# Attention with a top-32 mask and a maxout layer on one core: the first batch's values loaded later, their zero blocks written once, and new estimates in the planner

## The chip, the cores and the metric

The kernel runs on one core of one Trainium2 chip. A core has five engines that work side by side, each through its own list of instructions in the order in which they were written down: TensorE (PE, matrix products), VectorE (DVE), ScalarE (ACT), GpSimd (POOL) and SyncE (SP, which here only issues transfers, DMAs, between HBM and the on-chip memory). An instruction that waits for another engine holds up everything behind it on its own engine. The metric is the device time of one execution in microseconds (us).

## The reference

```
scores = q @ k^T / 8                       # 8 batches x 8 heads, 576 queries, 576 keys, 64 wide
kth    = 32nd largest score of each row
attn   = softmax(scores where scores >= kth, else -1e9)
x      = attn @ v                          # heads side by side: 4608 tokens x 512
h      = max(x @ w1, x @ w2, x @ w3)       # 512 -> 768
out    = h @ w_out                         # 768 -> 512
```

All inputs and the output are float32. The kernel splits float32 numbers into a high and a low half of 16 bits (or a rounded and a remaining part), and makes three products of halves where one float32 product is asked for.

## The kernel before, in words

**Attention.** A batch has four pairs of heads. For a pair, `load_qk` loads queries and keys by six DMAs; `prep` turns them on PE (lines 451 and 460), ACT brings them back (454, 464, 465) and POOL takes the remaining part (469). The 576 queries of a pair are five units: four of 128 queries for both heads and one of 64. A unit goes through some twenty steps: scores on PE (L508), copies by ACT (L519), the eight largest of each group of 72 scores on DVE (L536), a guess at the 32nd largest (L542 to L567), a sign pass on ACT (L574), a product on POOL (L579), a maximum pass on DVE (L583), the mask on DVE (L626), the exponential on ACT (L635), turned weights on PE (L693) and copies by ACT (L708). Every two units, PE multiplies the weights with the values (`values`, L738) and DVE scales the result (`scaled_x`, L748).

**Values.** `load_v` fills a tile `vt` of 128 x 10 x 64 numbers for a pair of heads by six DMAs from HBM (lines 400 to 405). Two half blocks of the tile must be zero, and two further DMAs (406, 407) copy them there from a tile `zeros`, at every load. `square_v` (ACT, L414) sums the squares of the values of each pair; when all four pairs of a batch are summed, `scale_v` makes the scale that L748 needs: a sum on DVE (L180), a product on PE (L184), a copy by ACT (L188) and three small steps on DVE (`powers`, 165 to 169).

**Weights.** 18 blocks of `w1`, `w2`, `w3` and `w_out` are loaded (L227), decoded by DVE in 30 pieces of three instructions (L240 to L242), squared by ACT (L252), summed by PE (L261), and cut into 16-bit halves in 48 pieces (POOL L298, ACT L301, POOL L304). From the second group of blocks on, a load needs the decoding of the block four places earlier.

**Expert layer.** For each batch, PE multiplies x with the three inner weights (L794) and h with the outer ones (L854). These products need all the weight cuts of their block and x of all four pairs. Their instructions stand in a second list, `fill`, from which the planner takes when PE has nothing better.

**The planner.** Every step is a `Piece` with an engine, an estimated duration, the pieces that it needs, and a rank. `in_order` simulates the five engines with these estimates and writes the pieces down one by one. For each engine it looks at pieces by rank (the window reaches `LEAD` = 8 ranks above the lowest that is left), and takes among those the first in rank whose estimated start is within `PATIENCE` of the earliest (0 for SP and ACT). A result is taken to be seen by another engine after the piece's duration plus `LATE` of the piece's engine plus 100 ns. So estimates, ranks and `LATE` set the order of each engine's list, and nothing else: on the chip the engines wait for each other by semaphores.

Unit n has rank n plus the offset of the step in `OFFSETS`; the loads of queries and keys have the rank of their first unit minus 3.5 (-3.5, -1.5, 0.5, 2.5 for the four pairs of the first batch, whose first units are 0, 2, 4, 6). Weight group i has rank `RANK_W[i]`, its loads at most `RANK_W[2]`. Loads of values have the rank of their pair's first unit plus `RANK_V` = -12.

Of the kernel before, what the change touches and what calls it, by code (L numbers as in the profile page):

```python
# [8 lines left out]
F32 = mybir.dt.float32  # L9
# [23 lines left out]
LEAD = 8.0  # L33
LOCK_A = -150.0
LOCK_B = -100.0
OFFSETS = {'x1': 0.96, 'j': 0.85, 'i': 0.48, 'N': 0.29, 'w1': -0.04, 'e1': -1.15, 'y': 0.91, 's1': 0.01, 'v': -0.12, 'u': -0.09, 'p1': -0.14, 'g0': 0.06}
RANK_P = -3.5
RANK_R = 4.0
AHEAD = 4
RANK_W = (-2.0, 1.0, 3.0, 5.0)  # L40
RANK_V = -12.0
RANK_M = -20.0
LATE = {'PE': 160.0, 'DVE': 85.0, 'ACT': 100.0, 'POOL': 40.0, 'SP': 2000.0}


class Piece:
# [86 lines left out]
def kernel(ctx, tc, q, k, v, moe_w1, moe_w2, moe_w3, moe_w_out, out):  # L133
    nc = tc.nc
    B, H, S, D = q.shape
    P = 128
# [11 lines left out]
    const = ctx.enter_context(tc.tile_pool(name="const", bufs=1))  # L148
    io = ctx.enter_context(tc.tile_pool(name="io", bufs=2))
# [63 lines left out]
    def load_weight(j):  # L213
        src, c, n, at0 = parts[j]
        if c % 2 == 0:
            raw = [wall.bitcast(I32)[:, 2 * CUT + at0:2 * CUT + at0 + 2 * n]]
        elif j < 3 * KC:
            raw = [wk.tile([P, n], I32, name=nm) for nm in ("xh", "xl")]
        elif j == len(parts) - 1:
            raw = [wk.tile([P, 2 * n], I32, name="ssb", bufs=NSSB)]  # L220
        elif j in raw_of:
            raw = raw_of[j]
        else:
            raw, raw_of[j + 2] = ([wk.tile([P, 2 * n], I32, name=nm)] for nm in ("xh", "xl"))
        m = 2 * n // len(raw)
        for k, t in enumerate(raw):
            nc.sync.dma_start(t, src[c * P:(c + 1) * P, :].bitcast(I32)[:, k * m:(k + 1) * m])  # L227
        raw_of[j] = raw
# [84 lines left out]
    def piece(engine, cost, run, needs=(), rank=0.0, takes=(), mode=None, alone=False):  # L313
        x = Piece(engine, cost, run, needs, rank, [(rings[r], rel) for r, rel in takes], mode, alone)
        pieces.append(x)
        return x

    def scale_pieces(parts_, needs, rank):
        a = piece("DVE", 55, parts_[0], needs, rank)
        rel = []  # L320
        b = piece("PE", 64, parts_[1], [a], rank, [("tr", rel)])
        c = piece("ACT", 40, parts_[2], [b], rank)
        rel.append(c)
        return piece("DVE", 200, parts_[3], [c], rank)
# [3 lines left out]
    def weights():  # L328

        decoded, loads, last_cut, staged_odd = {}, {}, [], []  # L330
        for i in range(4):
            mine = range(i * KC, (i + 1) * KC) if i < 3 else range(3 * KC, len(parts))
            rank = RANK_W[i]
            done = []
            release = []
            for j in mine:
                n = parts[j][2]

                free, c = [], parts[j][1]
                takes = [] if c % 2 == 0 else [("ssb", free)] if j == len(parts) - 1 else [("x", free)]  # L340
                needs = [decoded[j - AHEAD]] if j >= AHEAD else []
                if c % 2 and 3 * KC + 1 < j < len(parts) - 1:
                    takes, free = [], staged_odd[-1]
                    needs.append(loads[j - 2])
                loads[j] = piece("SP", 4100 if i < 3 else 2700, lambda j=j: load_weight(j), needs, min(rank, RANK_W[2]), takes)
                if c % 2:
                    staged_odd.append(free)
                    if j < len(parts) - 1:
                        before_x.append(loads[j])
                for j0 in range(0, n, PIECE[n]):  # L350
                    rel = []
                    x = piece("DVE", 1300 if i < 3 else 1800, lambda j=j, j0=j0: decode(j, j0),
                              [loads[j], *([decoded[j - 1]] if j else []), *([x] if j0 else [])], rank, [("ob", rel), ("ob", rel)])
                    rel.append(x)
                decoded[j] = x
                free.append(x)
                rel = []
                y = piece("ACT", 740, lambda j=j: square_w(j), [x], rank, [("junk", rel)])
                if i < 3:
                    z = piece("PE", 330, lambda j=j: sum_w(j), [y, *done[-1:]], rank, [("m", release)] * 2 if j % KC == 0 else [])  # L360
                    rel.append(z)
                    done.append(z)
                else:
                    rel.append(y)
                    done.append(y)
            if i < 3:
                scaled = piece("DVE", 1500, lambda i=i: column_scale(i), done, rank)
                release.append(scaled)
            else:
                scaled = scale_pieces(norm_scale("wo", lambda: wosq, const), done, rank)  # L370
                wo_scaled.append(scaled)
            for j in mine:
                for j0 in range(0, parts[j][2], CUT):
                    f = cut(j, j0)
                    rel = []
                    a = piece("POOL", 450, f[0], [scaled], rank, [("ws", rel)])
                    h = piece("ACT", 410, f[1], [a, *last_cut], rank)
                    lo = piece("POOL", 630, f[2], [h], rank)
                    rel.append(lo)
                    last_cut = [a, h]  # L380
                    lows[j, j0] = lo
# [2 lines left out]

    v_of, vs_of, sq_of, qk_of, T_of, at = {}, {}, {}, {}, {}, {}

    zeros = const.tile([P, D], F32, name="zeros")
    nc.gpsimd.memset(zeros, 0.0)


    def main_rows(t, b, h):
# [2 lines left out]
    def load_v(b, hp):  # L394


        vt = io.tile([P, 10, D], F32, name="vt", bufs=6)
        v0, v1 = (main_rows(v, b, 2 * hp + h) for h in range(2))
        last = v[at.get(b, b), 2 * hp:2 * hp + 2, MAIN:S]
        nc.sync.dma_start(vt[:, 0:NU, :], v0)  # L400
        nc.sync.dma_start(vt[0:64, 8, :], last[0])
        nc.sync.dma_start(vt[0:64, NU:2 * NU, :], v1[64:P])
        nc.sync.dma_start(vt[64:P, NU:2 * NU - 1, :], v1[0:64, 1:NU])
        nc.sync.dma_start(vt[64:P, 2 * NU - 1, :], last[1])
        nc.sync.dma_start(vt[64:P, 9, :], v1[0:64, 0])
        nc.sync.dma_start(vt[64:P, 8, :], zeros[64:P])
        nc.sync.dma_start(vt[0:64, 9, :], zeros[0:64])
        v_of[b, hp] = vt

    def square_v(b, hp):  # L410
# [5 lines left out]
    def scale_v(b):  # L416
        return norm_scale("v", lambda: sq_of.pop(b), sm, lambda: vs_of.update({b: scale_of["v"]}))
# [586 lines left out]
    scaled_v, loaded_v = {}, {}  # L1004
# [4 lines left out]
    def values_of(b):  # L1009

        done = []
        first = min(k for k, x in enumerate(units) if x[0] == b)
        for hp in early if b == 0 else range(NP):
            at_ = units.index((b, hp, 0))
            v_done[b, hp] = []
            x = loaded_v[b, hp] = piece("SP", 1600, lambda hp=hp: load_v(b, hp), rank=at_ + RANK_V, takes=[("vt", v_done[b, hp])])
            rel = []
            y = piece("ACT", 910, lambda hp=hp: square_v(b, hp), [x], first - 1.0, [("junk", rel)])
            rel.append(y)
            v_done[b, hp].append(y)  # L1020
            done.append(y)
        scaled_v[b] = scale_pieces(scale_v(b), done, first + 0.5)

    load_last, users = [], [[] for _ in preps]

    def prepare(pi):
        b, hp = preps[pi]
        rank = starts[pi] + RANK_P
        load = piece("SP", 3200, lambda: load_qk(b, hp), list(load_last), rank)
        box = {}  # L1030
        load_last.clear()
        done, last = [], list(load_bits)
        load_bits.clear()
        for k in range(3):
            def products(k=k):
                if k == 0:
                    box["turns"] = prep(b, hp)
                box["turns"][k][0]()
            rel = []
            x = piece("PE", 109 if k == 0 else 436, products, [load, *done[-1:]], rank, [("tr", rel)])  # L1040
            y = piece("ACT", 157 if k == 0 else 1100, lambda k=k: box["turns"][k][1](), [x, *last, *done[-1:]], rank)
            rel.append(y)
            load_last.append(x)
            if pi >= 2:
                users[pi - 2].append(x)
            done.append(y)
            if k:
                z = piece("POOL", 1364, lambda k=k: box["turns"][k][2](), [y], rank)
                done.append(z)
                load_bits.append(z)  # L1050
        prepared[pi] = done
# [60 lines left out]
    with tc.If(redo != 0):  # L1112
        with tc.For_i(0, B, 1) as b:
# [6 lines left out]
            for hp in range(NP):  # L1120
# [5 lines left out]
                for u in range(NU + 1):  # L1126
                    i = len(units)
# [52 lines left out]
```

## Time and profile before

| | |
|---|---|
| median of 3 runs | 1386.01 us (1384.56 to 1386.39) |
| profiled execution, device time | 1387.35 us |
| profiled execution, span from first to last instruction | 1385.6 us |
| PE busy | 1225.9 us (88%) |
| DVE busy | 1202.1 us (87%) |
| ACT busy | 1118.7 us (81%) |
| POOL busy | 992.7 us (72%) |
| mean granted TensorE clock | 0.965 |

The busy times are over the whole span, whose parts differ: the first 200 us hold the decoding of the weights beside the attention of the first units, then follows a long steady part, and the last 70 us hold the expert layer's end. A granted clock of 1.00 stands for TensorE's upper level (2.4 GHz), 0.50 for its lower one (1.2 GHz).

### The profile page before, as it was taken

How to read it: one execution, taken by the hardware profiler on the slowest of the kernel's cores; microseconds unless marked ns; L12 is line 12 of the kernel's file. 1: busy time of each engine (PE TensorE's matmuls, PEld its weight loads, DVE VectorE, ACT ScalarE, POOL GpSimd, SP SyncE). 2: the span in 40 equal slices, each digit the busy share in tenths (PEclk: the TensorE clock that was granted, in tenths of full speed). 3: DMA queues.
4: the chain of work that ended last, by engine and by line, in shares of the span. 5: the costliest groups of instructions: out<-in, count | busy, mean ns of one | idle time of the engine just before them, and what ended most of it. 6: DMA issues, size and time to landing. Idle time of an engine off the chain costs nothing.

```text
span 1385.6 us, 32482 instructions
## 1 busy us (share of the span) xinstructions
PE 1225.9 (88%) x9981; PEld 867.2 (63%) x9981; DVE 1202.1 (87%) x5928; ACT 1118.7 (81%) x2732; POOL 992.7 (72%) x1658
## 2 busy tenths in 40 slices
PE   0434489899889999999999999999999999999997
PEld 0222257577557676776667675777677766767775
DVE  1899689989989999999999899999999999999621
ACT  2556689988998889988997899899988998898622
POOL 1589877778776778777877787788777887777511
PEclk9997589989879999999999999999999999999999
DMA  4541001110110010101010201111111101000000
GB/s 145 172 139 52 1 18 36 49 41 19 52 28 18 26 45 19 43 19 53 19 53 1 68 21 33 29 46 26 36 37 34 45 23 37 19 17 1 17 17 26
DMA packets 113014, 54.75 MB, mean 40 GB/s; under 512 B 96960, under 2 KB 105152, under 8 KB 112832
## 3 DMA queue, kind: packets, MB, share of 16 engines
q1 hardware_dynamic: 112832, 52.59, 14.1%
q8 instruction: 81, 1.33, 0.4%
q14 instruction: 101, 0.83, 0.2%
HBM read 42.07 MB, written 9.44 MB: 37 GB/s over the span
## 4 chain that ended last, share of the span: by engine, by line
PE 58%; DVE 19%; ACT 13%; issue 3%; SPq 3%; POOL 3%; DMA 1%; ACTq 0%; DVEq 0%; POOLq 0%
PE m L794 24%; PE tr L738 9%; PE s L508 9%; PE tr L693 7%; PE m L854 6%; DVE L L536 5%; DVE ssb L626 3%; ACT pm L635 3%; DVE Q L583 2%; ACT pT L708 2%; ACT ssb L519 2%; ACT w L574 2%; DVE ob L241 2%; PE tr L460 1%; DVE wall L242 1%
## 5 line engine op out<-in xcount | busy, mean ns | idle before, releaser
L794 PE MATMUL m<-xh,wall 128*128 128x256 f16 (+2 forms) x2448 | 441.2, 280 | 1.2 <-DVE h L803 0.6
L579 POOL TENSOR_TENSOR w<-ssb,w 128x576 f32<-128x576 f32 x288 | 413.4, 1440 | 29.2 <-ACT w L574 25.2
L794 PEld LDWEIGHTS <-wall 128*128 128x128 f16 x3672 | 340.0, 98 | 85.7 <-issue 15.9
L794 PE MATMUL m<-xl,wall 128*128 128x256 f16 (+2 forms) x1224 | 336.0, 279 | 0.0
L536 DVE MAX8 L<-s 128x8 f32<-128x72 f32 x2048 | 306.3, 220 | 20.2 <-PE s L508 10.3
L626 DVE SCALAR_TENSOR_TENSOR ssb<-ssb,kth 128x576 f32<-128x576 f32 x288 | 262.0, 925 | 1.1
L635 ACT ACTIVATE pm<-ssb,nb 128x576 f32<-128x576 f32 x288 | 224.2, 779 | 44.2 <-DVE ssb L626 40.6
L508 PE MATMUL s<-kT,qT 64*128 64x288 f32 x1920 | 216.5, 338 | 30.5 <-ACT ssb L519 8.7
L574 ACT ACTIVATE w<-ssb,Q 128x576 f32<-128x576 f32 x288 | 222.9, 778 | 13.9 <-DVE Q L567 10.8
L693 PE MATMUL tr<-ident,pm 128*128 128x128 f32 x1152 | 186.6, 290 | 52.8 <-ACT pm L635 47.8
L583 DVE MAX8 Q<-w 128x8 f32<-128x576 f32 x288 | 214.6, 747 | 17.4 <-POOL w L579 17.4
L708 ACT COPY pT<-tr 128x512 f32<-128x512 f32 (+1 forms) x416 | 210.8, 521 | 20.0 <-PE tr L693 12.1
L508 PEld LDWEIGHTS s<-kT,qT 64*128 64x128 f32 x1920 | 146.0, 196 | 100.0 <-issue 26.2
L693 PEld LDWEIGHTS tr<-ident,pm 128*128 128x128 f32 x1152 | 134.6, 146 | 101.0 <-ACT pm L635 60.4
L738 PE MATMUL tr<-pT,vt 128*64 128x256 f32 (+1 forms) x1920 | 187.4, 344 | 0.8 <-ACT pT L708 0.5
L519 ACT COPY ssb<-s 128x576 f32<-128x576 f32 x256 | 161.0, 641 | 28.5 <-DVE L L536 13.2
L803 DVE SCALAR_TENSOR_TENSOR h<-m,rises,h 128x256 f32<-128x256 f32 (+2 forms) x204 | 100.1, 491 | 66.9 <-PE m L794 59.3
L738 PEld LDWEIGHTS tr<-pT,vt 128*64 128x64 f32 x1920 | 111.6, 142 | 65.6 <-issue 19.4
L809 POOL TENSOR_TENSOR hl<-h,hh 128x256 f16<-128x256 f32 (+2 forms) x102 | 82.0, 804 | 82.3 <-ACT hh L806 77.2
L854 PE MATMUL m<-wall,hh 128*128 128x512 f16 x432 | 128.8, 380 | 0.1
L642 POOL TENSOR_SCALAR den<-sums 128x2 f32<-128x2 f32 (+1 forms) x160 | 43.0, 269 | 83.9 <-ACT pm L635 75.6
L654 POOL TENSOR_SCALAR rsw<-rs 128x128 f32<-128x128 f32 x160 | 61.9, 387 | 38.7 <-DVE z L565 13.0
(123 smaller groups left out, 1865.7 us busy)
## 6 DMA issues: line engine op xcount, KB each, us to landing
qt<-in_q_dram SPq DMA_DIRECT2D x68, 128.0 KB, 2.8
kt<-in_k_dram SPq DMA_DIRECT2D x68, 128.0 KB, 2.9
out_dram<-ob SPq DMA_DIRECT2D x32, 256.0 KB, 2.3
wall<-in_moe_w_dram SPq DMA_DIRECT2D x6, 768.0 KB, 4.7
vt<-in_v_dram SPq DMA_DIRECT2D x32, 128.0 KB, 2.3
xh<-in_moe_w_dram SPq DMA_DIRECT2D x6, 384.0 KB, 5.0
xl<-in_moe_w_dram SPq DMA_DIRECT2D x6, 384.0 KB, 5.6
vt<-in_v_dram SPq DMA_DIRECT2D x32, 64.0 KB, 2.2
```

The source lines that it names most:

```text
L508: nc.tensor.matmul(s[:, h, :HALF], qT[sl, qa, c0:c0 + P], kT[sl, ka, i * HALF:(i + 1) * HALF], start=(n_ == 0), stop=(n_ == 2))
L536: nc.vector.max(d["L"][:, t, g, :], d["s"][i][:, t, g0:g0 + GW] if d["nt"] == 2 else d["ssb"][0][:, g * GW:(g + 1) * GW])
L574: nc.scalar.activation(d["w"][t], d["ssb"][t], AF.Sign, bias=d["Q"][:, t, 0:1], scale=-1.0, accum_out=d["cnt"][:, t:t + 1])
L579: nc.gpsimd.tensor_tensor(d["w"][t], d["ssb"][t], d["w"][t], ALU.mult)
L583: nc.vector.max(d["Q"][:, t, 1:NW], d["w"][t])
L626: nc.vector.scalar_tensor_tensor(ss, ss, d["kth"][:, t:t + 1], ss, ALU.is_lt, ALU.subtract, accum_out=d["lost"][:, t:t + 1])
L635: nc.scalar.activation(d["pm"][:, t], d["ssb"][t], AF.Exp, bias=d["nb"][:, t:t + 1], scale=-1.0 / SHRINK, accum_out=d["sums"][:, t:t + 1])
L693: nc.tensor.transpose(pt[:, j * P:(j + 1) * P], pm[:, i, 64 * i + j * P:64 * i + (j + 1) * P], ident)
L708: nc.scalar.copy(pT[:, 512 * i:512 * i + m] if i < 2 else pT[:, 8 * P:10 * P], pt[:, :m])
L738: nc.tensor.matmul(xp[64 * h:64 * h + 64, :m], vt[:, 4 * h + i if i < 4 else 8 + h, :], keys(i, h), start=(i == 0), stop=(i == 4))
L794: nc.tensor.matmul(box["ps", i][:, :c1 - c0], a, bb[:, kc, c0:c1], start=(kc == 0 and k == 0), stop=(kc == KC - 1 and k == 2))
L854: nc.tensor.matmul(box["po"][:n], a[:, f, cs], bb, start=(f == 0 and k == 0), stop=(f == FC - 1 and k == 2))
```

## The change

The first batch's values get their own rank offset, `RANK_V0` = 0.0 in place of -12, and the scale made from them moves from rank 0.5 to 4.0. The tile `vt` is no longer taken from a rotating pool: six fixed tiles are made at the start, and the zero half blocks of each are written there once by POOL; the two DMAs per load and the tile `zeros` go. The planner's estimates of loads change (values 1600 to 3800 ns, queries and keys 3200 to 4000, weights 4100 to 5000 and 2700 to 3400), the ranks of the weights change, `LATE` goes from 160 to 79 for PE and from 40 to 98 for POOL, and three offsets change or are new: `e1` (the second copy of the scores by ACT), `h` (the choice of the threshold on DVE) and `E2` (the last copy of turned weights by ACT).

```diff
-OFFSETS = {..., 'e1': -1.15, ..., 'g0': 0.06}
+OFFSETS = {..., 'e1': -1.05, ..., 'g0': 0.06, 'h': -0.01, 'E2': 0.48}
...
-RANK_W = (-2.0, 1.0, 3.0, 5.0)
+RANK_W = (-2.0, 0.0, 1.0, 4.0)
 RANK_V = -12.0
+RANK_V0 = 0.0
...
-LATE = {'PE': 160.0, 'DVE': 85.0, 'ACT': 100.0, 'POOL': 40.0, 'SP': 2000.0}
+LATE = {'PE': 79.0, 'DVE': 85.0, 'ACT': 100.0, 'POOL': 98.0, 'SP': 2000.0}
...
-                loads[j] = piece("SP", 4100 if i < 3 else 2700, lambda j=j: load_weight(j), needs, min(rank, RANK_W[2]), takes)
+                loads[j] = piece("SP", 5000 if i < 3 else 3400, lambda j=j: load_weight(j), needs, min(rank, RANK_W[2]), takes)
...
-    zeros = const.tile([P, D], F32, name="zeros")
-    nc.gpsimd.memset(zeros, 0.0)
+    which_v = [0]
+    vts = [const.tile([P, 10, D], F32, name=f"vt{i}") for i in range(6)]
+    for t in vts:
+        nc.gpsimd.memset(t[64:P, 8, :], 0.0)
+        nc.gpsimd.memset(t[0:64, 9, :], 0.0)
...
-        vt = io.tile([P, 10, D], F32, name="vt", bufs=6)
+        vt = vts[which_v[0] % len(vts)]
+        which_v[0] += 1
...
-        nc.sync.dma_start(vt[64:P, 8, :], zeros[64:P])
-        nc.sync.dma_start(vt[0:64, 9, :], zeros[0:64])
...
-            x = loaded_v[b, hp] = piece("SP", 1600, lambda hp=hp: load_v(b, hp), rank=at_ + RANK_V, takes=[("vt", v_done[b, hp])])
+            x = loaded_v[b, hp] = piece("SP", 3800, lambda hp=hp: load_v(b, hp), rank=at_ + (RANK_V if b else RANK_V0), takes=[("vt", v_done[b, hp])])
...
-        scaled_v[b] = scale_pieces(scale_v(b), done, first + 0.5)
+        scaled_v[b] = scale_pieces(scale_v(b), done, first + (0.5 if b else 4.0))
...
-        load = piece("SP", 3200, lambda: load_qk(b, hp), list(load_last), rank)
+        load = piece("SP", 4000, lambda: load_qk(b, hp), list(load_last), rank)
```

## Rows read from the trace of the kernel before

**Rows 1.** Windows of stretches: busy us (instructions) of PE, PEld, DVE, ACT, POOL; granted clock; DMA.
```profile
0.00:100.00 100.00, 31.73 (x140) 20.95 (x140) 67.31 (x215) 43.71 (x84) 47.03 (x68) 1.00 0.50 158
...
100.00:200.00 100.00, 50.77 (x283) 31.43 (x283) 82.32 (x354) 70.37 (x169) 86.36 (x134) 0.73 0.10 24
...
200.00:1312.00 1112.00, 1077.15 (x8896) 764.70 (x8895) 1038.07 (x5321) 988.87 (x2442) 850.14 (x1440) 0.98 0.12 32
...
300.00:400.00 100.00, 88.65 (x688) 59.92 (x686) 94.42 (x486) 89.05 (x221) 82.25 (x134) 0.92 0.13 32
...
1300.00:1386.00 86.00, 78.26 (x789) 59.95 (x787) 21.93 (x64) 23.43 (x62) 14.59 (x32) 0.99 0.05 18
```

**Rows 2.** Timeline of SP: start us, us, queue, line, DMA issued, count, idle before.
```profile
0.75 0.40 SPq L400 DMA_DIRECT2D vt<-in_v_dram  x1
...
20.02 0.59 SPq L407 DMA_DIRECT2D vt<-zeros  x1
...
20.66 1.29 SPq L424 DMA_DIRECT2D qt<-in_q_dram  x2
...
24.68 0.59 SPq L227 DMA_DIRECT2D wall<-in_moe_w_dram  x1
...
40.48 0.33 SPq L227 DMA_DIRECT2D xl<-in_moe_w_dram  x1
...
52.18 1.25 SPq L424 DMA_DIRECT2D qt<-in_q_dram  x2
...
63.32 0.33 SPq L227 DMA_DIRECT2D xl<-in_moe_w_dram  x1
...
76.84 1.26 SPq L424 DMA_DIRECT2D qt<-in_q_dram  x2
```

**Rows 3.** Timeline of DVE: start us, us, line, operation, count, idle before.
```profile
22.77 0.16 DVE L180 TENSOR_REDUCE s<-sq 128x1 f32<-128x4 f32 x1 [21.30 <-ACT junk L414]
...
29.25 1.37 DVE L240 TENSOR_SCALAR ob<-wall 128x384 int32<-128x384 int32 x1 [5.05 <-DMA wall<-in_moe_w_dram]
...
53.04 0.35 DVE L240 TENSOR_SCALAR ob<-wall 128x384 int32<-128x384 int32 x1
...
121.75 0.47 DVE L748 SCALAR_TENSOR_TENSOR xs<-tr,down_v,pT 128x256 f32<-128x256 f32 x1
...
166.49 0.76 DVE L583 MAX8 Q<-w 128x8 f32<-128x576 f32 x1 [7.58 <-POOL w L579]
```

**Rows 4.** Timeline of ACT, first 10 us.
```profile
6.88 1.28 ACT L414 ACT_TABLE_LOAD   x1 [6.88 <-DMA vt<-zeros]
...
8.18 0.74 ACT L414 ACTIVATE junk<-vt 128x640 bf16<-128x640 f32 x1
```

**Rows 5.** Timeline of PE around its first scores, first values and first expert products.
```profile
35.27 0.80 PE L261 MATMUL m<-junk,ones_b 128*128 128x384 bf16 x2 [6.83 <-ACT junk L252]
...
35.99 1.81 PE L508 MATMUL s<-kT,qT 64*128 64x288 f32 x12
...
113.49 4.52 PE L738 MATMUL tr<-pT,vt 128*64 128x256 f32 x20
...
200.83 0.63 PE L794 MATMUL m<-xh,wall 128*128 128x256 f16 x2
```

**Rows 6.** Timeline of POOL, end of the first preparation.
```profile
30.36 1.51 POOL L469 TENSOR_TENSOR qT<-raws,qT 128x576 fp32r<-128x576 f32 x1
```

**Rows 7.** Windows as in Rows 1, just before the granted clock falls.
```profile
115.00:120.00 5.00, 3.68 (x22) 1.68 (x18) 4.96 (x13) 1.63 (x4) 3.81 (x6) 1.00 0.54 131
```

**Rows 8.** Line L693 on PE in 20:121 and 200:280: ns min/median/max, first and last start.
```profile
L693 PE MATMUL tr<-ident,pm x16: 421/421/477, 92.1 to 107.6; 128*128 128x128 f32 x16
...
L693 PE MATMUL tr<-ident,pm x72: 272/273/329, 207.7 to 274.5; 128*128 128x128 f32 x72
```

**Rows 9.** Line L241 on DVE in 28:52 and 52:134: ns min/median/max, first and last start.
```profile
L241 DVE SCALAR_TENSOR_TENSOR ob<-wall,ob x4: 557/559/1635, 30.7 to 43.5; 128x384 int32<-128x384 int32 x4
...
L241 DVE SCALAR_TENSOR_TENSOR ob<-wall,ob x11: 559/730/1658, 53.4 to 126.8; 128x384 int32<-128x384 int32 x8, 128x512 int32<-128x512 int32 x3
```

More of the change, by code (lines that the diff above doesn't have):

```diff
@@ L35 @@
 LOCK_B = -100.0
-OFFSETS = {'x1': 0.96, 'j': 0.85, 'i': 0.48, 'N': 0.29, 'w1': -0.04, 'e1': -1.15, 'y': 0.91, 's1': 0.01, 'v': -0.12, 'u': -0.09, 'p1': -0.14, 'g0': 0.06}
+OFFSETS = {'x1': 0.96, 'j': 0.85, 'i': 0.48, 'N': 0.29, 'w1': -0.04, 'e1': -1.05, 'y': 0.91, 's1': 0.01, 'v': -0.12, 'u': -0.09, 'p1': -0.14, 'g0': 0.06, 'h': -0.01, 'E2': 0.48}
 RANK_P = -3.5
```

## The prediction, made before the changed kernel ran

> **What bounds the kernel now.** I read the windows first, since the busy shares of the whole span mix three regimes. In 200 to 1312 us PE is busy 1077 of 1112 us (96.9%) and DVE 93.4% of it: PE is full, DVE nearly so, and the order of the lists can win little and lose some [rows 1]. In 1300 to 1386 us PE still has 78 us of work and DVE 22: the kernel ends on PE's expert products. In the first 200 us PE is busy only 82.5 us. So PE has 117.5 us to spare there and almost none afterwards; its first expert product starts at 200.83 us [rows 5], and from there to the end it hardly stops. What lets that first product start earlier moves the end by the same amount, as long as the steady part stays as full.
>
> What holds the first 200 us is then the question, and SP's timeline answers for the beginning: SP issues the 32 DMAs of the four value tiles (four times the eight of lines 400 to 407), one every 0.64 us, from 0.75 to 20.6 us, and only then the first queries, at 20.66, and the first weights, at 24.68 [rows 2]. DVE has nothing of weight until the first weight block lands: its first decoding starts at 29.25 us, released by that DMA [rows 3]. Behind it DVE hardly rests: 67.31 us of the first 100, of which 70.75 were left when it began, 95% [rows 1]. So the path to PE's first expert product is: 19.9 us of issues for values that nobody needs yet, six issues of queries and keys, a weight block, and then DVE's and POOL's load of decoding, cutting and eight units of attention.
>
> **The change, part by part.**
>
> *Values behind queries, keys and weights.* By rank, SP's list now begins with the first queries and keys (-3.5), the first weight group (-2) and the second pair's queries and keys (-1.5); the values come at 0, 2, 4 and 6, between the later weights. The first query's issue moves from 20.66 to about 0.75 us: 19.91 us [rows 2]. Everything that follows on SP to the first weight block is the same list as before, so the first decoding should start at 29.25 - 19.91 = 9.34 us. Term: -19.9 us. It is the whole of the prediction, so the covers matter:
>
> - The 24 remaining issues of values (24 x 0.62 = 14.9 us at the pace of rows 2) must go somewhere. SP stands idle between the last issue at 40.48 and the one at 52.18 (11.4 us after the issue itself) and between 63.32 and 76.84 (13.2 us) [rows 2], together 24.6 us, and the values have no wait of their own. What of them is put before the second weight group delays that group: DVE first decodes it at 53.04 [rows 3], against the last of its first three issues at 40.48, with some 5 us for landing (the first block of all took 29.25 - 24.68 = 4.57 us). That leaves 7 to 8 us of slack, and two value tiles take 7.4. So below nothing is excluded (nothing is shortened by it), and the upper end is all 14.9 us. I take 1.0 us, near the lower end, because the idle stretches are longer than the issues.
> - The values are first used by L738 at 113.49 and their scale by L748 at 121.75 us [rows 5, 3], 93 and 102 us after the shift. Even if all 14.9 us came behind the issue that now stands at 76.84 (56.9 after the shift [rows 2]), they would be out by 73 us. Nothing is late there.
> - ACT's four squares (0.74 us each [rows 4] and a short readout) and the four small DVE steps of the scale (0.16 us by the first [rows 3]) lay in time in which both engines waited. They now fall where DVE is full: 4 x 0.16 = +0.6 us. ACT has room (43.7 us busy of the first 100 [rows 1]): 0, and at most 4 x 0.74 = 3.0 us.
> - ACT's table load, 1.28 us, stood before the first square while queries were far off [rows 4]. It now stands before the first copy of turned keys. Its cover: POOL is done with the first pair's remainders at 30.36 + 1.51 = 31.87 us [rows 6], but the first scores stand behind L261 on PE, which starts only at 35.27 [rows 5]. 3.4 us of slack against 1.28: 0; without the cover 1.28.
>
> *Zeros written once.* Twelve POOL writes at the start replace 64 DMAs. The second remainder begins at 30.36 us [rows 6], the first one of the same size some 1.5 us earlier; 19.9 us earlier that is 9 us, and twelve writes of small blocks before it, at even 0.3 us each, are 3.6 us: 0. The eight of these DMAs in the first 20 us would be worth 8 x 0.64 = 5.1 us by themselves, but they stand in the 32 that move, and are counted there. The other 56 stand in SP's list of the steady part, where the end is PE's: 0. If a fixed tile had to wait longer than one from a pool, SP alone would wait, between loads that are a batch ahead.
>
> *Estimates, LATE, ranks, offsets.* They cost no instruction; they rewrite the order of every list. What an order is worth is bounded by the windows: the poorest full window, 300 to 400, has PE at 88.65%, against 96.9% in the mean: 8.2 us for one such window [rows 1]. One more or one fewer is what I allow: -8 to +8 us. I take 0, for no row says which way. In the beginning one stall shows what an order can win: DVE waits 7.58 us up to 166.49 for a product that POOL has placed behind a run of weight cuts [rows 3].
>
> Sum: 1387.35 - 19.9 + 1.0 + 0.6 = 1369.05 us for the profiled execution (span 1385.6 and 1.75 around it). The median of the runs is 1.34 us lower than that execution, so the time is 1369.05 - 1.34 = 1367.7 us, 18.3 us (1.3%) below the median.
>
> *Two rules of the Trainium skill weighed.* The granted clock stands at 1.00 up to 120 us [rows 7] though PE does very little; the mean over 100 to 200 is 0.73 [rows 1]. Read as it stands, work that now runs just after 120 us at the lower level would run before it and faster: PE's 50.77 us of 100 to 200 hold about 20% of that stretch in the 20 us concerned, 10 us, of which 1 - 272/421 = 35% would be saved, some 3.5 us at most. But the same transpose (L693) takes 421 ns at 92 to 108 us and 272 ns after 200 [rows 8], so PE ran at the lower level all along, and the column's 1.00 isn't the clock of that stretch. By the Trainium skill, "TensorE: Matmul & The Clock Gate" (The HAM clock gate), the throttled state is the default and activity lifts it; the durations agree, the column doesn't, and by that rule this term is 0. I go by the durations: 0.
>
> A decoding step (L241) takes 557 ns at the least before 52 us, with POOL nearly idle, and 730 ns in the median, 1658 at the most, beside POOL's cuts [rows 9]. The Trainium skill, "SBUF — State Buffer" (two separate sides), says that a DVE instruction with two SBUF inputs and a GpSimd instruction exclude each other for whole instructions. Were the decodings, now ranked earlier, to run ahead of POOL's cuts, the (730 - 559) ns of each would come back: over the 22 pieces after 52 us and two such instructions in each, 22 x 2 x 0.17 = 7.5 us. It is part of the third rival.
>
> **The rivals.**
> 1. *The values come between DVE and its weights.* SP's estimates (5.0 us for a weight block whose issues take about 1.1) make the planner think SP is the slow one; if all four value tiles are written down ahead of loads that DVE then waits for, two of them cost 7.4 us and four 14.9: 1375 to 1382.6, say 1378. For it: values at rank 0 come before the second weight group, also at 0. Against it: 24.6 us of idle time on SP.
> 2. *The steady part gets worse.* The new LATE and offsets let ACT or DVE stand in front of late results, and PE runs dry. Its place is 200 to 1312 us; it decides from 18.3 us of additional idle time on PE, 1.6% of that stretch, or a little over two windows like 300 to 400. Three of them: 3 x 8.2 = 24.6, so 1367.7 + 24.6 = 1392, slower. For it: DVE at 93.4% and PE at 96.9% leave each other little room. Against it: the same planner and same pieces; LATE moves by 81 and 58 ns, against pieces of hundreds.
> 3. *The beginning shortens by more.* The stall of 7.58 us goes and the decodings meet fewer cuts (up to 7.5 us by rows 9): 1367.7 - 7.6 - 3.7 (half of that) = 1356.
> 4. *It doesn't do what it says.* The planner takes the values first after all, because SP takes whatever could start earliest and the values wait for nothing; only the eight zero DMAs go: 1386 - 5.1 = 1381. Against it: the first queries and the first weights wait for nothing either, and stand before the values by rank.
>
> **How the numbers follow.** Forecast (1360 to 1376) 0.55; first rival 0.17; second 0.08; third 0.14; fourth 0.06. Two runs of this kernel can be told apart at about 0.2%, 2.8 us: faster is below 1383.2, slower above 1388.8. The forecast, the third, nearly all of the first and of the fourth are faster: 0.88. Within 0.2% is what lies between, 0.05; slower is nearly all of the second, 0.07. The forecast's bounds are 1367.7 - 8 and + 8; the range that leaves out 2 in 10 at most takes in the third rival below and most of the first and fourth above: 1353 to 1383.
>
> **What would show it.** SP's first issue is a query, near 0.75 us, and DVE's first decoding starts at 9 to 10 us. PE's first expert product starts near 182 us, and PE is still about 97% busy from there to the end. If the decoding starts at 9 but the first expert product not before 190, the first rival or POOL's cuts took it back; if that comes at 182 and the end doesn't follow, the second did. The prediction is wrong if the time is over 1383 or the first decoding over 15 us.

## The result, and the profile after

| | time, us (median, range) | ratio to before, 95% interval |
|---|---|---|
| before, in the same series | 1385.82 (1382.45 to 1386.39) | 1 |
| after | 1373.02 (1369.32 to 1375.52) | 0.9913 [0.9896, 0.993] |

The change makes the kernel 0.9% faster, 12.8 us by the medians. The forecast was 18.3 us. The profiled execution of after took 1373.02 us, its median, with a span of 1371.2 us, 14.4 us less than the span before, whose profiled execution is 1.5 us above its median; the accounts below are made between these two profiles.

The windows of after (columns as in [rows 1]):

```profile
0.00:100.00 100.00, 33.88 (x143) 20.85 (x143) 79.67 (x261) 49.05 (x95) 59.54 (x98) 0.88 0.51 159
100.00:200.00 100.00, 56.06 (x414) 39.69 (x415) 81.94 (x378) 78.58 (x192) 88.59 (x134) 0.76 0.12 28
300.00:400.00 100.00, 81.26 (x620) 54.75 (x617) 90.40 (x471) 86.85 (x215) 74.85 (x125) 0.88 0.10 25
181.82:1300.00 1118.18, 1076.18 (x8939) 765.09 (x8936) 1042.96 (x5347) 991.19 (x2455) 848.30 (x1448) 0.98 0.12 31
1300.00:1372.00 72.00, 63.67 (x647) 47.97 (x645) 13.39 (x38) 14.80 (x37) 8.83 (x17) 0.98 0.07 21
```

DVE gets 12.4 us more done in the first 100 us than in [rows 1]: that is the earlier start. But 300 to 400, the poorest full window before, is now poorer: PE 81.26 us against 88.65. Part of that is only place: a stretch in which PE runs short of expert products, described below, lies almost wholly in this window now and reached beyond it before. Over the long part PE is busy for 96.2% (1076.18 of 1118.18) against 96.9%.

SP's timeline of after (columns as in [rows 2]) begins with the queries; one pair's values come at 15.68, the third issue of the second weight group at 21.35, its last at 33.93, and the next values not before 85.70:

```profile
0.74 1.38 SPq L427 DMA_DIRECT2D qt<-in_q_dram  x2
...
4.84 0.59 SPq L228 DMA_DIRECT2D wall<-in_moe_w_dram  x1
...
15.68 0.59 SPq L405 DMA_DIRECT2D vt<-in_v_dram  x1
...
21.35 0.33 SPq L228 DMA_DIRECT2D xl<-in_moe_w_dram  x1
...
33.93 0.33 SPq L228 DMA_DIRECT2D xl<-in_moe_w_dram  x1
...
85.70 0.42 SPq L405 DMA_DIRECT2D vt<-in_v_dram  x1
```

DVE's timeline of after: the first decoding at 9.41 us (29.25 in [rows 3]), the second group's at 39.85 without a wait (53.04), a stall of 7.60 us of a kind that stood elsewhere before, and the first scaled x of the values:

```profile
9.41 1.47 DVE L241 TENSOR_SCALAR ob<-wall 128x384 int32<-128x384 int32 x1 [7.94 <-DMA wall<-in_moe_w_dram]
...
39.85 0.35 DVE L241 TENSOR_SCALAR ob<-wall 128x384 int32<-128x384 int32 x1
...
57.56 0.17 DVE L650 RECIPROCAL rs<-den 128x2 f32<-128x2 f32 x1 [7.60 <-POOL den L645]
...
141.90 0.48 DVE L751 SCALAR_TENSOR_TENSOR xs<-tr,down_v,pT 128x256 f32<-128x256 f32 x1 [2.29 <-PE tr L741]
```

PE's timeline of after: a stand of 23.23 us before the sum for the scale of `w_out` (the sum on DVE before it reads `wosq`), the first expert product (200.83 in [rows 5]), and the first expert product of the second batch, which stood at 414.63 before:

```profile
122.95 0.59 PE L185 MATMUL tr<-s,ones 128*128 128x1 f32 x2 [23.23 <-DVE s L181]
...
181.82 0.38 PE L797 MATMUL m<-xh,wall 128*128 128x256 f16 x2
...
402.18 0.38 PE L797 MATMUL m<-xh,wall 128*128 128x256 f16 x2
```

So the beginning is 19.84 us shorter at DVE and 19.01 at PE, and the end only 14.4. The stretch between the two first expert products, in before, in after and in the kernel of the first experiment below (windows, columns as above), shows where the difference stays:

```profile
200.83:414.63 213.80, 194.64 (x1523) 136.28 (x1522) 193.93 (x1007) 190.34 (x473) 165.01 (x274) 0.91 0.15 37
```

```profile
181.82:402.18 220.36, 192.04 (x1552) 134.56 (x1550) 200.34 (x1045) 193.03 (x482) 165.95 (x284) 0.93 0.12 30
```

```profile
181.60:392.04 210.44, 190.00 (x1543) 133.76 (x1540) 197.51 (x1032) 192.26 (x482) 168.57 (x286) 0.94 0.13 33
```

PE's idle time in this stretch is length less busy time: 19.2 us before, 28.3 after, 20.4 with the loads alone. The account at the second batch's first product: -19.01 (earlier start) + 9.16 (more idle) - 2.60 (less busy) = -12.45 us, which is 402.18 - 414.63. From there to the end it is 971.0 us before and 969.0 after: the end follows this product. The stretch has a hole by its nature. In after the last inner product of the first batch ends at 323.34 us and the last outer one at 345.16, and until 402.18 PE has attention alone to do. That part in before, in after and with the loads alone:

```profile
344.96:414.63 69.67, 56.72 (x383) 36.59 (x381) 60.94 (x325) 63.54 (x159) 54.00 (x89) 0.80 0.16 40
```

```profile
345.16:402.18 57.02, 38.28 (x284) 26.70 (x283) 49.48 (x276) 51.02 (x126) 40.75 (x69) 0.79 0.11 27
```

```profile
338.72:392.04 53.32, 39.16 (x285) 26.43 (x285) 51.03 (x268) 50.32 (x126) 44.39 (x76) 0.84 0.12 30
```

The hole is shorter in after than before, but PE stands in it for 18.7 us, against 13.0 before and 14.2 with the loads alone: 5.8 of the 9.16 us. In after nearly all of it ends with a result of ACT (waits of PE in this part that ACT ended: 17.1 us, 10.6 before). The two largest rows (engine, what waited, who released it, us in total, times, longest), before and after:

```profile
PE tr L693 <- ACT pm L635: 5.2, 4, 4.2
PE s L508 <- ACT ssb L519: 3.9, 2, 3.2
```

```profile
PE s L511 <- ACT ssb L522: 7.3, 4, 3.3
PE tr L696 <- ACT pm L638: 4.3, 2, 2.3
```

### The profile page after: what moved, and what is told of

Same layout as the page of the kernel before. It is cut to its first block, busy times and chain, and to the rows that moved or that the text cites. A ratio compares the mean times of both kernels' runs of the same rounds, so it can differ in the third digit from the quotient of the medians.

```text
span 1371.2 us, 32398 instructions
## 1 busy us (share of the span) xinstructions
PE 1212.2 (88%) x9981; PEld 859.8 (63%) x9981; DVE 1200.0 (88%) x5928; ACT 1115.9 (81%) x2732; POOL 989.1 (72%) x1669
## 4 chain that ended last, share of the span: by engine, by line
PE 60%; DVE 19%; ACT 13%; POOL 3%; issue 3%; SPq 1%; DMA 0%; ACTq 0%; DVEq 0%; POOLq 0%
PE m L797 24%; PE tr L741 9%; PE s L511 9%; PE m L857 8%; PE tr L696 7%; DVE L L539 6%; DVE ssb L629 3%; ACT pm L638 3%; ACT w L577 3%; DVE Q L586 2%; ACT pT L711 2%; ACT ssb L522 2%; PE tr L463 2%; DVE ob L242 1%; PE tr L691 1%
## 5 line engine op out<-in xcount | busy, mean ns | idle before, releaser
L539 DVE MAX8 L<-s 128x8 f32<-128x72 f32 x2048 | 307.3, 223 | 19.9 <-ACT ssb L522 9.9
L629 DVE SCALAR_TENSOR_TENSOR ssb<-ssb,kth 128x576 f32<-128x576 f32 x288 | 257.1, 908 | 1.0
L511 PE MATMUL s<-kT,qT 64*128 64x288 f32 x1920 | 210.8, 334 | 32.6 <-ACT ssb L522 16.5
L696 PE MATMUL tr<-ident,pm 128*128 128x128 f32 x1152 | 182.0, 287 | 26.4 <-ACT pm L638 19.2
L511 PEld LDWEIGHTS s<-kT,qT 64*128 64x128 f32 x1920 | 144.3, 194 | 96.9 <-ACT ssb L522 28.5
L741 PE MATMUL tr<-pT,vt 128*64 128x256 f32 (+1 forms) x1920 | 183.2, 338 | 3.3 <-ACT pT L716 2.0
L812 POOL TENSOR_TENSOR hl<-h,hh 128x256 f16<-128x256 f32 (+2 forms) x102 | 78.1, 766 | 75.3 <-ACT hh L809 73.0
```

The costliest lines, as they stand in the source:

```text
L511: nc.tensor.matmul(s[:, h, :HALF], qT[sl, qa, c0:c0 + P], kT[sl, ka, i * HALF:(i + 1) * HALF], start=(n_ == 0), stop=(n_ == 2))
L539: nc.vector.max(d["L"][:, t, g, :], d["s"][i][:, t, g0:g0 + GW] if d["nt"] == 2 else d["ssb"][0][:, g * GW:(g + 1) * GW])
L629: nc.vector.scalar_tensor_tensor(ss, ss, d["kth"][:, t:t + 1], ss, ALU.is_lt, ALU.subtract, accum_out=d["lost"][:, t:t + 1])
L696: nc.tensor.transpose(pt[:, j * P:(j + 1) * P], pm[:, i, 64 * i + j * P:64 * i + (j + 1) * P], ident)
L741: nc.tensor.matmul(xp[64 * h:64 * h + 64, :m], vt[:, 4 * h + i if i < 4 else 8 + h, :], keys(i, h), start=(i == 0), stop=(i == 4))
```

## The experiments

The question at the start was whether the moved first issues are the whole gain and the planner's new numbers (estimates, ranks of the weights, `LATE`, offsets) take part of it back, or whether every part gives its share and what is missing is lost with any earlier start; each expectation names its theories. Each kernel was timed in five rounds beside before. Before's own median lies between 1382.95 and 1385.82 us in the different series, so where two kernels of different series are compared the ratios decide. "First product" is PE's first expert product, "second product" the second batch's first, both from the profile.

| kernel | median, us | ratio to before, 95% | first product | second product | span |
|---|---|---|---|---|---|
| after | 1373.02 | 0.9913 [0.9896, 0.993] | 181.8 | 402.2 | 1371.2 |
| e1_loads_only | 1363.28 | 0.9855 [0.984, 0.987] | 181.6 | 392.0 | 1361.7 |
| e2_zeros_only | 1376.96 | 0.9963 [0.9949, 0.9976] | 194.6 | 405.1 | 1375.0 |
| e4_old_numbers | 1365.24 | 0.9863 [0.9848, 0.9878] | 182.1 | 394.5 | 1368.2 |
| e5_old_late | 1375.44 | 0.9941 [0.9927, 0.9954] | 189.6 | 405.2 | 1370.9 |
| e6_old_e1 | 1370.24 | 0.9902 [0.9885, 0.9919] | 183.1 | 402.8 | 1370.0 |
| e7_new_e1_alone | 1364.73 | 0.9858 [0.9837, 0.9879] | 181.2 | 393.8 | 1362.6 |
| e8_old_loads_weights | 1378.47 | 0.9963 [0.9948, 0.9979] | 190.9 | 398.2 | 1377.2 |
| e9_old_steps | 1373.65 | 0.9926 [0.991, 0.9942] | 189.3 | 407.4 | 1371.5 |
| e10_more_dve | 1373.32 | 0.9923 [0.991, 0.9937] | 182.0 | 399.2 | 1369.2 |
| e11_more_pe | 1376.65 | 0.9941 [0.9924, 0.9958] | 183.4 | 408.8 | 1375.7 |
| e12_cut_estimates | 1384.02 | 0.9989 [0.9979, 1.0] | 195.6 | 411.0 | 1381.9 |
| e13_best | 1386.79 | 1.0017 [1.0007, 1.0027] | 193.3 | 409.4 | 1382.2 |

The profile of e4 is of its slowest execution (its range is 1363.08 to 1369.99), so its median and not its span is used. Each profile is one execution: that of e6 is 1.5 us above the median of its kernel, those of e5, e10 and e13 are 2.8, 2.3 and 2.7 us below theirs. A difference of a few us between two profiles is therefore not yet one between two kernels.

**The moved loads alone**: before, with

```diff
+RANK_V0 = 0.0
-            ... rank=at_ + RANK_V, ...
+            ... rank=at_ + (RANK_V if b else RANK_V0), ...
-        scaled_v[b] = scale_pieces(scale_v(b), done, first + 0.5)
+        scaled_v[b] = scale_pieces(scale_v(b), done, first + (0.5 if b else 4.0))
```

> The kernel before with one edit: the first batch's values at rank offset 0 and their scale at rank 4; the zero blocks are still copied by DMAs, and all estimates, LATE, weight ranks and offsets are the old ones. Theory A (the shift is the moved loads alone, and the 4.6 us that the changed kernel lost behind its first expert product come from the new numbers of the planner): first decoding at 9 to 10 us, first expert product at 181 to 185, from there to the end 1185 as in the kernel before, time 1366 to 1370. Rival B (an earlier start by itself makes PE run dry later, since the attention can't feed it): first expert product the same, but 1189 or more from there to the end, time 1371 to 1375.

It is 1.45%, 20.1 us, faster than before, more than the whole change. These few edits bring everything that the change brings, and what comes with them in the change costs.

**The zeros alone**: before, with six fixed tiles and without the two DMAs.

```diff
-        nc.sync.dma_start(vt[64:P, 8, :], zeros[64:P])
-        nc.sync.dma_start(vt[0:64, 9, :], zeros[0:64])
```

> The kernel before with one edit: six fixed value tiles whose zero blocks POOL writes once, no zero DMAs; the values are still loaded first. Theory A: eight of the 32 first issues go, 5.1 us; first decoding at 24.1 us, first expert product at 195.7, time 1381. Rival: the order of the rest of the list decides, and a shift of 5 us at the start is lost in it: first decoding at 24.1, time 1386 (no change). That the 56 later zero DMAs cost anything would show as a time under 1379.

5.1 us (0.37%) faster, with the first decoding 4.98 us earlier, at 24.27: the eight DMAs of zeros among the first 32, as worked out in the prediction. The time lies under the 1379 us that the expectation named as the sign of a cost of the 56 later ones, but before itself was 1383.7 us in this series and not 1386.0; by the ratio, which allows for that, no such cost is shown.

**The change with the old numbers**: after, with the offsets, `LATE`, `RANK_W` and all estimates of loads as before.

```diff
-OFFSETS = {..., 'e1': -1.05, ..., 'h': -0.01, 'E2': 0.48}
+OFFSETS = {..., 'e1': -1.15, ...}
-RANK_W = (-2.0, 0.0, 1.0, 4.0)
+RANK_W = (-2.0, 1.0, 3.0, 5.0)
-LATE = {'PE': 79.0, ..., 'POOL': 98.0, ...}
+LATE = {'PE': 160.0, ..., 'POOL': 40.0, ...}
...
```

> The changed kernel with all the planner's old numbers (LATE, offsets, weight ranks, estimates of loads); values behind and zeros once stay. Theory A: as e1, first decoding near 9.4 us, first expert product at 181 to 185, 1185 us from there to the end, 1366 to 1370: better than the changed kernel, whose new numbers cost some 5 us. Rival B: 1371 to 1375, like the changed kernel, with 1189 us behind the first expert product. Rival C (the new estimates are needed for the start, because the old ones place the values between DVE and its weights): first expert product at 188 or later.

Its ratio is that of the loads alone, and its interval doesn't meet that of after. So the new numbers cost 0.5%, about 7 us by the ratios (7.8 by the medians), and the zeros bring nothing once the values no longer stand in front.

**The old `LATE` alone**: after, with `LATE` 160 for PE and 40 for POOL.

```diff
-LATE = {'PE': 79.0, ..., 'POOL': 98.0, ...}
+LATE = {'PE': 160.0, ..., 'POOL': 40.0, ...}
```

> The changed kernel with LATE as before (PE 160, POOL 40). If LATE is what cost the 4.6 us behind the first expert product: 1185 us there, and 1368. If not: 1189 and 1373. First expert product at 180 to 184 either way; POOL placing weight cuts ahead of small steps that DVE waits for (DVE's stall of 7.6 us at 50 to 57.6 us in the changed kernel) may come or go with POOL's figure.

The first product comes 7.8 us later than in after, and the stretch from there to the end is 8.1 us shorter (1181.3 us against 1189.4); the intervals of the two ratios overlap. By these profiles, of which that of e5 is its fastest execution, `LATE` moves time from one place to the other. The old `LATE` doesn't bring the 7 us back, so `LATE` isn't by itself the loss.

**The offset of ACT's second score copy**, taken back in after, and put into the loads alone. Its reason was a row of PE's waits in the long part (engine, what waited, who released it, us in total, times, longest), in before, after and the loads alone:

```profile
PE s L508 <- ACT ssb L519: 5.5, 7, 3.2
```

```profile
PE s L511 <- ACT ssb L522: 13.3, 15, 3.3
```

```profile
PE s L509 <- ACT ssb L520: 8.8, 12, 3.9
```

PE's scores wait for ACT to copy out the ones before; the new offset puts that copy later. The edits:

```diff
-OFFSETS = {..., 'e1': -1.05, ...}
+OFFSETS = {..., 'e1': -1.15, ...}
```

> The changed kernel with one number put back: offset e1 (ACT's second copy of the scores) at -1.15 in place of -1.05. Theory A1 (the copy ranked later lets PE's next scores wait for it: 13.3 us of PE's waits in the long part of the changed kernel against 5.5 before): PE's wait for that copy falls to 6 to 9 us, its idle time behind the first expert product from 49.5 to some 42, and the time to 1364 to 1368. Rival A2 (it is one of the other numbers, or their sum): PE's wait stays at 11 to 15 us and the time at 1371 to 1375.

```diff
-OFFSETS = {..., 'e1': -1.15, ...}
+OFFSETS = {..., 'e1': -1.05, ...}
```

> The kernel before with the values loaded behind (1363.3 us) and offset e1 at -1.05. Theory A1: the number alone costs the 5 to 8 us: PE waits 13 us or more for the copy of the scores, 1368 to 1372. Rival A2: it costs nothing alone, 1362 to 1365.

The same row in the one and in the other:

```profile
PE s L511 <- ACT ssb L522: 12.7, 15, 3.3
```

```profile
PE s L509 <- ACT ssb L520: 8.6, 11, 3.9
```

With the old offset the wait stays at 12.7 us and the time within after's interval; with the new one alone it stays at 8.6 and the time at that of the loads alone. That theory has fallen: the wait follows the lists, not this offset.

**Two halves of the numbers**: after with the old estimates and `RANK_W`, and after with the old offsets and `LATE`.

```diff
-RANK_W = (-2.0, 0.0, 1.0, 4.0)
+RANK_W = (-2.0, 1.0, 3.0, 5.0)
-    ... piece("SP", 5000 if i < 3 else 3400, ...
+    ... piece("SP", 4100 if i < 3 else 2700, ...
...
```

> The changed kernel with the old estimates of loads and the old weight ranks; LATE and the three offsets are the new ones. If LATE and offsets cost the time: as the changed kernel behind its first expert product (1189 us there), 1370 to 1375. If estimates and weight ranks do: 1181 to 1186 us there and 1363 to 1368, with the first expert product near 182.

```diff
-OFFSETS = {..., 'e1': -1.05, ..., 'h': -0.01, 'E2': 0.48}
+OFFSETS = {..., 'e1': -1.15, ...}
-LATE = {'PE': 79.0, ..., 'POOL': 98.0, ...}
+LATE = {'PE': 160.0, ..., 'POOL': 40.0, ...}
```

> The changed kernel with the old LATE and the old offsets; the estimates of loads and the weight ranks are the new ones. If LATE and offsets cost the time behind the first expert product: 1181 to 1186 us there. If the estimates and weight ranks cost the start with the old LATE, as the run with the old LATE alone showed (first expert product at 189.6): again 188 to 191, and 1370 to 1376 in all; if not, 182 and 1364 to 1368.

| | old loads and weights | new loads and weights |
|---|---|---|
| old offsets and `LATE` | 1365.2 (e4) | 1373.7 (e9) |
| new offsets and `LATE` | 1378.5 (e8) | 1373.0 (after) |

Each half costs by itself, the two do not add, and the best corner is the old one (ratios 0.9863, 0.9926, 0.9963 and 0.9913). In e8 the second product is at 398.2, earlier than in after, and yet the end comes later: 979 us from there, against 964 to 974 in all other kernels. Of these 10 us more than in after 7.2 are PE's busy time, 955.0 us against 947.8 with the same work (8033 and 8035 instructions); the granted clock reads 0.91 in 680 to 720, where after has 1.00. So the loss isn't in one place in all of them.

**More work for DVE and more for PE** in the stretch between the two products, since both engines stand there longer than with the loads alone (DVE 20.0 us against 12.9, PE 28.3 against 20.4; before, 19.9 and 19.2). Into after went ten more searches on DVE, or twice the transposes of ten units on PE:

```diff
+        if 24 <= n < 34:
+            nc.vector.max(more, d["ssb"][0])
```

> The changed kernel with ten more DVE maxima of 128 x 576 (0.75 us each, 7.5 us), one beside the threshold's choice in each of the units 24 to 33, their results unused; all lists keep their order. These units lie in the stretch of about 323 to 402 us in which PE has no expert product. Theory D (up to the second batch's first expert product the kernel is bound by DVE, with 343 us of work in every version; its idle time there, 49.5 us in the changed kernel against 42.1 before, is the lost time): that product starts 5 to 8 us later than 402 and the time is 1378 to 1381. Rival E (PE bounds it, by its late start and idle time): within 2 us of 402, time 1371 to 1375.

```diff
-        for j in range(4):
+        for j in (*range(4), *(range(4) if 24 <= n < 34 else ())):
```

> The changed kernel with four more transposes into the same place in each of the first two turns of the units 24 to 33 (20 groups of some 0.6 us at the upper clock, 12 us of PE work, results the same); all lists keep their order. Theory D: PE's 18.7 us of idle time in that stretch take most of it: second batch's first expert product at 402 to 406, time 1373 to 1377. Rival E: all 12 us show, 1384 to 1387.

The added searches ran in the stretch (line, operation, count: ns min/median/max, first and last start us), and the stretch of that kernel by windows:

```profile
L610 DVE MAX8 more<-ssb x10: 743/748/751, 290.7 to 362.3; 128x8 f32<-128x576 f32 x10
```

```profile
182.00:399.16 217.16, 188.94 (x1551) 133.04 (x1549) 202.44 (x1055) 193.02 (x482) 165.46 (x284) 0.94 0.12 31
```

and the stretch of the kernel with more for PE:

```profile
183.40:408.80 225.40, 202.55 (x1624) 145.86 (x1622) 201.51 (x1045) 193.53 (x482) 165.03 (x284) 0.92 0.12 30
```

The added searches took 7.5 us (10 x 0.748). The second product came 3.0 us earlier all the same, and the time is that of after within its interval. But this execution was ahead before the first addition. DVE's choice of unit 24's threshold, in after and in this kernel:

```profile
295.47 0.15 DVE L606 TENSOR_REDUCE kth<-oh 128x1 f32<-128x9 f32 x1
```

```profile
290.68 0.15 DVE L608 TENSOR_REDUCE kth<-oh 128x1 f32<-128x9 f32 x1
```

Of a lead of 4.8 us 3.0 were left at the second product, so in this pair of executions the searches cost about 1.8 us of their 7.5. The lead was no work of theirs: up to this point the two kernels have the same lists. One piece of it shows how it can arise. In after a small step of DVE begins 0.05 us behind the start of a pass of POOL and ends with it; in the other kernel it begins 0.04 us behind the same pass and is done in a tenth of the time (POOL and DVE, in after and in this kernel):

```profile
215.59 1.41 POOL L582 TENSOR_TENSOR w<-ssb,w 128x576 f32<-128x576 f32 x1
215.64 1.39 DVE L568 SCALAR_TENSOR_TENSOR z<-n,b 128x8 f32<-128x8 f32 x1
```

```profile
215.81 1.46 POOL L582 TENSOR_TENSOR w<-ssb,w 128x576 f32<-128x576 f32 x1
215.85 0.14 DVE L568 SCALAR_TENSOR_TENSOR z<-n,b 128x8 f32<-128x8 f32 x1
```

PE's 10.5 us more (202.55 - 192.04) moved the second product by 6.6 us and the span by 4.5; this execution was 0.3 us behind after at the same threshold, so about 6.3 us of the 10.5 show in the second product. The ratio rose by 0.28%, 3.9 us, and the two intervals still touch (0.9924 to 0.993), so that size is uncertain. What is shown is that the stretch isn't full of DVE's work, and that it is more sensitive to PE's list: 22.9 us of idle time are left instead of 28.3. It isn't shown that PE's own work bounds it. The added transposes also stand in front of the copies by ACT that every unit waits for, and ACT, busy 51.02 of the 57.02 us without expert products and the one for which PE mostly waits there, was not given more work; nor was POOL.

**Estimates nearer to the trace.** The planner counts POOL's two steps of a weight cut (L299, L305 in after) at 450 and 630 ns; the trace of after has a mean of 673 ns for 36 of the 48 first steps and 477 for the other twelve, and 822 for the second step; the new estimates are the means of before (725 for the 36, 787). POOL was late in the stall of 7.60 us. The same edit went into after and into the loads alone:

```diff
-                    a = piece("POOL", 450, f[0], [scaled], rank, [("ws", rel)])
+                    a = piece("POOL", 725, f[0], [scaled], rank, [("ws", rel)])
-                    lo = piece("POOL", 630, f[2], [h], rank)
+                    lo = piece("POOL", 787, f[2], [h], rank)
```

> The changed kernel with the planner's estimates of the two POOL steps of a weight cut at what the trace of the kernel before shows, 725 and 787 ns in place of 450 and 630. If DVE's stall of 7.6 us at 50 to 57.6 us (a denominator placed behind a run of cuts on POOL) comes from the cuts being estimated too short: the stall is under 3 us, the second batch's first expert product at 393 to 397, time 1364 to 1368. Rival: the new order has its own stalls of the same size, 1370 to 1376.

> The kernel before with the values loaded behind (1363.3 us) and the same two estimates of weight cuts, as a try at a version better than all others. By theory D the time follows DVE's idle time up to the second batch's first expert product (39.2 us with the values behind alone): with 35 us or less 1355 to 1360, with more than 42 us 1366 or more.

Both became slower: by the ratios 0.76% and 1.62%, 10.5 and 22.4 us (11.0 and 23.5 by the medians). Both decode their first weights at 10 us like their parents, and start the first product 14 and 12 us later. DVE's timeline in the first of them:

```profile
59.26 0.17 DVE L650 RECIPROCAL rs<-den 128x2 f32<-128x2 f32 x1 [4.35 <-POOL den L645]
...
134.29 0.48 DVE L751 SCALAR_TENSOR_TENSOR xs<-tr,down_v,pT 128x256 f32<-128x256 f32 x1 [4.03 <-PE tr L741]
...
141.74 0.48 DVE L751 SCALAR_TENSOR_TENSOR xs<-tr,down_v,pT 128x256 f32<-128x256 f32 x1 [6.97 <-PE tr L741]
```

and in the second:

```profile
124.50 0.29 DVE L555 MAX8 n<-nA 128x8 f32<-128x32 f32 x2 [5.17 <-POOL nA L543]
...
149.48 0.48 DVE L749 SCALAR_TENSOR_TENSOR xs<-tr,down_v,pT 128x256 f32<-128x256 f32 x1 [5.77 <-PE tr L739]
```

The wait on `den` shrinks from 7.60 to 4.35 us, which is what the edit was for, and DVE waits 4 to 7 us for PE's values and POOL's part of the search instead. The e13 kernel has the loads in their new place and is as slow as before: an order can cost the whole gain.

## Why the prediction was right, and where not

- *Values behind queries, keys and weights, -19.9.* Shown. The first query's issue is at 0.74 (20.66 in [rows 2]), the first decoding 9.41, the first expert product 181.82, where the prediction had "near 182". The loads alone moved the whole time by 20.1 us. The sum for everything but the planner's numbers is e4's time: 19.0 us below before by the ratio, forecast 18.3.
- *Values' other issues, +1.0, and the small DVE steps, +0.6.* Too small to see; the first product is 0.7 us earlier than these terms allow (200.83 - 18.3 = 182.5).
- *"Nothing is late there".* Wrong, and no price shows. SP puts the other three pairs' values behind the last weights, at 85.70 us and later, where the prediction had all of them out by 73. The first scaled x comes at 141.90 instead of 101.9 (121.75 in [rows 3] less 19.9). PE's stand of 23.23 us before 122.95 isn't for the values: it waits there for the scale of `w_out`; its wait for the scale of the values is 4.2 us, up to 135.75. The lateness cost the first expert product nothing that shows: the later three pairs' scaled x start at 150.5, 161.9 and 179.4 us against 156.4, 178.5 and 195.3 before, the last of them 2.4 us ahead of that product, and the loads alone, which have the first scaled x at 116.33, begin theirs at 181.60.
- *ACT's table load and the zeros' writes, 0.* Right in price, but the table load's cover was another one. It ran while ACT had nothing at all to do:

```profile
0.74 1.28 ACT L457 ACT_TABLE_LOAD   x1 [0.74 <-PEq L1167]
```

- *Zeros, 5.1 alone and nothing behind the moved loads.* Shown by e2 and e4.
- *Estimates, `LATE`, ranks, offsets: 0.* This is the term that was mis-sized, and the reason why 12.8 us came instead of 18.3: about +7 us (after against e4), inside its -8 to +8 but not at the 0 that was taken. As bounds on an order they were too narrow: the kernels with the loads in their new place that differ in the planner's numbers run from 0.9855 to 1.0017 of before, 22.4 us. What the prediction took from one window, 8.2 us, is no bound for an order that also shapes the first 200 us.
- *"From there to the end it hardly stops"*, so that an earlier first product moves the end as much. That failed in one stretch. PE has no expert product between 345.16 and 402.18 us in after and stands for 18.7 of these 57.0 us; before it was 13.0 of 69.7 us and with the loads alone 14.2 of 53.3. There the order of the attention's steps counts in full. The time from the first product to the end became 1189.4 us instead of 1184.8, and 1180.1 with the loads alone.
- *The rivals.* The first (values between DVE and its weights) isn't seen: one pair's values do stand ahead of the second group, but the group's first three issues are out by 21.7 us, its last by 34.3, and DVE decodes at 39.85 without a wait. The second (the steady part gets worse) is what took the 7 us: from the first expert product to the end PE stands for 49.5 us against 42.2 before, 7.3 us more, where 18.3 would decide. Of the third, the stall of 7.58 us at 166.49 [rows 3] went and one of 7.60 came at 57.56; the 30 decodings took 64.0 us of DVE's time against 65.3, not up to 7.5 less. The fourth is excluded by SP's first row.

What stays open is which detail of the lists makes PE stand in the stretch. It isn't the `e1` offset (e6, e7), not `LATE` by itself (e5), and for the most part not a load of DVE (e10); e8 and e9 show that either half of the numbers can lose 8 to 13 us without the other. The waits point at ACT's list, which no run changed or loaded by itself, apart from `e1`.

The fastest version run is the moved loads alone: 1363.28 us, 0.9855 of before. That is 0.58%, 8.0 us, below after by the ratios (9.7 by the medians), and its interval lies below that of after.

## What to carry to other kernels

Time before the first useful load is gained in full when the first engine in the chain waits for nothing else, and a look at the issuing queue's timeline gives its size to within 1 us. A change that also alters a planner's numbers should be timed in its parts: here a one-place edit was worth more than the whole, and estimates nearer to the trace made it up to 1.6% slower. A busy share of 97% over a long part doesn't say that every stretch of it is full; look for the stretch in which the filling work is missing, because a gain made ahead of it has to pass through it. And where work is added to find the limit, compare the two traces at the first addition too: here a lead of 4.8 us from elsewhere made 7.5 us of work look free.

## What was not expected of the hardware

The granted clock's column reads 1.00 until its first fall, and that fall doesn't mark a change of PE's speed. In 60 to 65 us e4 and the loads alone have the same 1.89 us of PE work in eight instructions; the granted clock (third figure from the right) reads 0.58 in the one and 1.00 in the other:

```profile
60.00:65.00 5.00, 1.89 (x8) 0.87 (x7) 5.00 (x15) 2.27 (x4) 3.13 (x4) 0.58 0.81 192
```

```profile
60.00:65.00 5.00, 1.89 (x8) 0.88 (x7) 4.97 (x16) 2.08 (x4) 3.13 (x4) 1.00 0.71 154
```

In after it falls at about 78 us (window 75 to 80), though the transposes before that already take 421 ns, the time of the lower level in [rows 8] (ns min/median/max, first and last start):

```profile
75.00:80.00 5.00, 1.37 (x6) 0.75 (x7) 4.90 (x18) 2.87 (x6) 5.00 (x6) 0.59 0.00 0
```

```profile
L696 PE MATMUL tr<-ident,pm x16: 417/421/477, 40.6 to 71.2; 128*128 128x128 f32 x16
```

A transpose of the same size takes the same time where the column does read the lower level (line of PE, and the window around it):

```profile
87.25 0.42 PE L691 MATMUL tr<-ident,pm 128*128 128x128 f32 x1
```

```profile
85.00:90.00 5.00, 2.06 (x9) 1.13 (x9) 4.90 (x19) 3.69 (x8) 4.80 (x8) 0.50 0.99 354
```

So ahead of its first fall the durations tell the level, 1.2 GHz here, and the column doesn't. The Trainium skill, "TensorE: Matmul & The Clock Gate" (The HAM clock gate), has the throttled state as the default; these durations agree with it.
